# A layer of long convolution and FFN: the last rows stored as 384 and 256 columns, twelve more warm-up products, four row turns issued by ScalarE's queue, and a new order

## The chip, the cores and the metric

The kernel runs on one core of a Trainium2 chip. The metric is the device time of one execution in microseconds, as the median of several runs. Engines are named as the profile names them: PE is TensorE (matmul; PEld is its weight load), DVE is VectorE, ACT is ScalarE, POOL is GpSimd, SP is SyncE, which here only issues DMAs. ScalarE and GpSimd can issue DMAs too; such an instruction stands in the engine's own queue, and what stands behind it waits for it.

## The reference

The inputs are bf16. q, k, v and x are 2048 x 640 (q and x are the same array); the weights of the FFN are 640 x 1728, 640 x 1728 and 1728 x 640.

```
ks = 4                                     # A: long convolution with gates
k_shift = causal convolution of k with shift_k (4 taps a channel)
kv = k_shift * v
y  = irfft(rfft(kv, 2S) * rfft(ssm_k, 2S))[:S] + kv * ssm_D
h  = x + layernorm(x) * y
h2 = h + (silu(n @ w_gate) * (n @ w_up)) @ w_down,   n = layernorm(h)
```

## The kernel before

The sequence is cut into four blocks of 512, and each block into four rows of 128 (one row has one sequence position per partition). The long convolution is done with DFTs of 1024 as matrix products, one per block: the spectra of kv and of the convolution's kernel are formed, multiplied and summed over pairs of blocks, and turned back. Then come the gate, the second layernorm and the FFN of the block.

A block's work has these stages, each with its name in the plan: loads of g (the convolution's kernel), k, v and x; `g` and `k`, where these are turned so that channels lie on partitions (DMA transposes L429 and L520, or PE transposes L539 in block 0), the four taps as products with diagonal matrices (L564) and the product with v; `X` and `G`, the spectra (products L344 of 320 columns, evictions L333); `h`, the window of two spectra; `m`, multiply and add on VectorE (L631, L658); `n`, the first layernorm's statistics (L669, L711, on ScalarE) and norm (L687); `i`, the inverse (VectorE steps L738 to L773, products L793, gate L807 and residual L820); `t`, the second layernorm applied (L719 on VectorE or L722 on ScalarE) and the rows turned (`turn_h`); `f`, the FFN of the block: gate and up products of 512 columns (L903, L980), evictions into sg on ScalarE (L963, with the gate's activation, and L969), products of these on VectorE (L971, L968, L990), and the down products of 320 columns (L1019), a row of 640 columns being a PSUM tile of two halves.

**Row turns.** In blocks 1, 2 and 3 (`HTURN`) the normalised row goes through a DMA transpose into its quarter of the tile hT (L833); in block 0 TensorE transposes it (L840) and ScalarE evicts (L842). The FFN's products L903 read all four quarters at once. In before SP issues every DMA transpose of the kernel, as all other hardware-queue DMAs but the very first (the taps' load).

**The end of a row in the FFN.** In blocks 0, 1 and 2 ScalarE evicts a row (L1025) and GpSimd adds it onto the output by DMA (L1026); with L1025 the row's PSUM tile comes free. In block 3 VectorE adds the row and h (L1035, or L1037 for a part), and SP stores it (L1039). The very last row is done in parts, so that less is behind the last product: 320, 160 and 160 columns (`LASTCUT`, L1005 and L1006), the last parts in a second PSUM tile.

**The order.** Every piece of work is an operation of a plan with a number, an engine and its buffers. The list `ORDER` gives the order in which they are issued (913 of them), and so the order in each engine's queue; buffers are taken from fixed pools in that order (4 PSUM tiles, 11 big tiles, 6 rows, 8 spectra; a row is free again when its turn has landed). A negative number -n-1 is operation n on its other engine (an eviction on VectorE in place of ScalarE). Nothing is reordered at run time; an engine that has to wait holds up all that stands behind.

**Warm-up.** TensorE begins with products of constants (`spin`, L1059) in three groups of 14, 16 and 8 (`WARMUP`): until the taps come, behind the turned taps (L1066), and behind the transposes of k (L539).

SP stops at the end until every DMA has landed (L1209), and then all engines meet.

Of the kernel before, what the change touches and what calls it, by code (L numbers as in the profile page):

```python
# [17 lines left out]
D = 640  # L18
FF = 1728
P = 128  # L20
# [31 lines left out]
WARMUP = (14, 16, 8)  # L52
# [9 lines left out]
LASTCUT = True  # L62
DIAGDVE = 4
ORDER = [
    1, 0, 4, 2, 3, 5, 7, 12, 8, 13, 9, 6, 15, 11, 14, 10, 27, 28, 23, 16, 127, 24, 122, 32, 124, 121, 17, 18, 19, 25, -27, 29, 31,
    -31, 33, -35, 20, 39, -41, 126, 36, -38, 21, 42, 35, 218, 41, 189, 123, 184, -44, 125, 44, 58, 190, 59, 79, 38, 80, 62, -64,
    45, 81, 60, -47, 64, 120, 75, 188, 128, 82, 47, -62, 66, 22, 65, 76, 51, 182, 77, -49, 54, 67, 68, -53, 78, 83, 387, 55, 49,
    187, 84, 261, 260, 53, 186, -70, 389, 56, -51, 71, 85, 96, -58, -73, -87, 100, 97, 73, 70, 101, -75, 262, 92, -94, 98, 99, 87,
    102, 103, 129, 132, 88, 89, 94, 95, 104, 105, 90, 108, 112, 185, 421, 91, 131, 130, 109, 106, 116, 113, 107, 110, 133, 134,
    117, 388, 111, 336, 191, 118, 137, 195, 319, 192, 119, 114, 193, 197, 196, 391, 203, 115, 199, 198, 211, 141, 135, 194, 207,  # L70
    204, 138, 205, 136, 200, 208, 201, 139, 209, 212, 206, 140, 210, 213, 214, 147, 202, 222, 318, 142, 159, 144, 145, 223, 148,
    151, 300, 215, 152, 146, 150, 143, 162, 160, 156, 219, 310, 163, 309, 149, 161, 225, 157, 164, 158, 153, 167, 301, 220, 154,
    166, 168, 396, 224, 155, 165, -227, 299, 398, 399, 221, 227, 397, 228, 229, 390, 243, 244, 169, 231, 235, 230, 239, 232, 217,
    -171, 236, 233, 240, 234, 237, 238, -180, -174, 245, -177, 246, 216, 241, 248, 180, 181, 177, 178, 174, 602, 175, 251, 171,
    249, 172, 263, 400, 264, 394, 311, 242, 266, 247, 395, 312, 303, 302, 253, 304, 305, 183, 265, 259, 315, 255, 256, 306, 313,
    402, 327, 401, 406, 307, 250, 252, 308, 320, 254, 407, 314, 267, 328, 356, 392, 316, 317, 257, 408, 409, 258, 321, 324, 337,
    323, 410, 354, 414, 403, 355, 415, 404, 411, 322, 416, 405, 601, 417, 412, 330, 413, 425, 325, 345, 418, 268, 329, 426, 428,
    332, 420, 333, 326, 331, 431, 334, 600, 429, 269, 422, 432, 335, 271, 280, 457, 346, 427, 270, 277, 273, 278, 423, 424, 274,
    419, 433, 430, 275, 348, 283, 603, 607, 347, 351, 454, 357, 284, 272, 281, 456, 279, 285, 339, 443, 434, 455, 435, 609, 338,
    349, 444, 458, 606, 342, 436, 437, 276, 350, 608, 459, 460, 447, 445, 340, 352, 341, 393, 610, 446, 289, 438, 611, 359, 448,  # L80
    523, 343, 344, 439, 449, 461, 450, 358, 451, 287, 440, 441, 282, 442, 286, 288, 360, 513, 361, 363, 367, 522, 473, 382, 383,
    353, 364, 368, 512, 452, 290, 372, 362, 297, 469, 298, 640, 365, 366, 616, 617, 373, 384, 618, 291, 385, 463, 369, 370, 620,
    619, 374, 624, 377, 625, 621, 295, 293, 453, 378, 375, 292, 626, 622, 462, 465, 470, 464, 467, 474, 623, 379, 294, 296, 612,
    376, 524, 687, 627, 613, 527, 466, 604, 468, 614, 380, 605, 525, 526, 650, 615, 644, 690, 628, 528, 529, 514, 477, 475, 689,
    647, 651, 632, 540, 371, 652, 532, 381, 648, 472, 531, 478, 516, 471, 515, 518, 541, 517, 568, 641, 519, 645, 630, 642, 787,
    533, 785, 629, 649, 536, 534, 691, 476, 631, 646, 569, 542, 686, 535, 493, 570, 633, 567, 549, 643, 520, 530, 480, 479, 485,
    521, 550, 537, 481, 538, 482, 543, 634, 545, 490, 484, 487, 546, 494, 491, 692, 495, 544, 635, 559, 547, 539, 483, 486, 488,
    496, 571, 492, 497, 657, 658, 498, 572, 688, 548, 653, 573, 574, 558, 659, 654, 489, 637, 551, 552, 655, 660, 553, 575, 555,
    639, 730, 554, 656, 576, 636, 561, 666, 560, 500, 556, 595, 502, 674, 501, 557, 596, 729, 499, 577, 564, 562, 731, 563, 578,
    590, 784, 591, 503, 510, 506, 508, 676, 739, 638, 509, 565, 786, 767, 766, 566, 662, 748, 507, 504, 663, 579, 597, 667, 673,  # L90
    511, 661, 664, 505, 592, 749, 665, 668, 669, 593, 675, 670, 678, 386, 671, 677, 598, 740, 672, 580, 581, 585, 757, 586, 582,
    587, 680, 769, 588, 768, 758, 771, 770, 772, 773, 774, 872, 744, 827, 742, 741, 583, 743, 735, 685, 679, 589, 733, 682, 745,
    793, 746, 732, 734, 750, 681, 736, 737, 776, 584, 775, 753, 845, 751, 747, 683, 794, 760, 759, 817, 795, 796, 693, 684, 873,
    754, 599, 777, 778, 738, 781, 874, 763, 752, 694, 695, 762, 755, 863, 788, 707, 780, 761, 844, 756, 710, 779, 696, 702, 764,
    697, 713, 782, 699, 853, 704, 703, 698, 714, 789, 711, 700, 705, 862, 594, 712, 718, 715, 719, 802, 706, 716, 818, 701, 708,
    709, 826, 765, 783, 717, 797, 720, 725, 807, 835, 798, 726, 803, 790, 791, 812, 721, 723, 724, 813, 792, 808, 727, 799, 728,
    722, 814, 815, 816, 804, 871, 809, 805, 819, 820, 829, 800, 801, 828, 823, 832, 836, 821, 822, -825, 847, 864, 865, 868, 825,
    849, 846, 850, 848, 810, 830, 831, 833, 854, 806, 838, 866, 858, 867, 834, 851, 855, 852, 857, 869, 837, 841, 870, 856, 875,
    859, 860, 861, 840, 877, 839, -843, 880, 881, 876, 899, 901, 843, -879, 902, 879, 882, 883, 889, 894, 895, 896, 897, 890, 891,
    892, 884, 905, 885, 893, 898, 908, 909, 886, 900, 887, 903, 906, 888, 910, 911, 904, 907, 912, 913, 811]  # L100
# [33 lines left out]
class Op:  # L134
    def __init__(self, n, eng, ns, fn, name, bufs, deps):
        self.n, self.eng, self.ns, self.fn, self.name, self.bufs, self.deps = n, eng, ns, fn, name, bufs, deps
        self.other = self.rest = None


class Plan:  # L140
    TOOK = {8: 9, 128: 13, 256: 18, 320: 21, 512: 28.5, 640: 33, 1024: 47, 1280: 57, 4096: 160, 5120: 199}
# [39 lines left out]
    def schedule(self, order):  # L181
# [3 lines left out]
        for n in order:  # L185
            op = self.ops[n if n >= 0 else ~n]
            assert op not in done and op.deps <= done
            done.add(op)
            if n < 0:
                op.eng, op.ns, op.fn = op.other  # L190
                if op.rest:
                    op.rest.fn = None
            for b in op.bufs:
                if b.tag is not None and b.at is None:
                    b.at = idle[b.tag].pop(0)
            for b in op.bufs:
                b.left -= 1
                if b.left == 0 and b.tag is not None:
                    idle[b.tag].append(b.at)
# [5 lines left out]
def kernel(ctx: ExitStack, tc: tile.TileContext, A_q, A_k, A_v, A_shift_k, A_ssm_k, A_ssm_D, B_x,  # L205
# [50 lines left out]
    def load(nbytes, packet, fn, w, r=()):  # L256
        return plan.moved("sp", nbytes, packet, fn, r, w)

    def transfer(nbytes, fn, r, w, eng="turn"):
        return plan.moved(eng, nbytes, 256, fn, r, w)  # L260
# [161 lines left out]
    def g_turned(g, drow=None):  # L422
        gT = new("t4")
        if plan.block in GTURN:
# [3 lines left out]
            for r in range(R):  # L428
                transfer(MB / 4, lambda r=r: nc.sync.dma_start(  # L429
                    out=ap(gT)[:, r, :].rearrange("p (c q) -> p c q", c=KT),  # L430
                    in_=ap(by_r).rearrange("q a b -> q (a b)")[:, r * D:(r + 1) * D], transpose=True), [by_r], [(gT, r)])
# [83 lines left out]
    def load_k(j):  # L515
        if j in KTURN or not j and K0TURN:
            kT = new("kT")
            for r in range(R):
                q, e = (nc.scalar, "aturn") if not j and r % 2 else (nc.sync, "turn")
                transfer(MB / 4, lambda r=r, q=q: q.dma_start(  # L520
                    out=ap(kT)[:, :, r, PAD:], in_=block(kk, j)[:, r, :], transpose=True), [], [(kT, r)], e)
# [304 lines left out]
    def turn_h(x, stats):  # L826
        hT = new("hT")
        for r, s in [(r, s) for s, rs in stats for r in rs]:
# [3 lines left out]
            if plan.block in HTURN:  # L832
                transfer(MB / 4, lambda hn=hn, at=at: nc.sync.dma_start(  # L833
                    out=ap(hT)[:, :, at * P:(at + 1) * P], in_=ap(hn), transpose=True), [hn], [(hT, r)])
# [11 lines left out]
    def load_w(gi):  # L846
# [24 lines left out]
        for i, (to, src, lo, n) in enumerate(parts):  # L871
            load(P * KT * n * 2, 2 * n, lambda to=to, src=src, lo=lo, n=n: nc.sync.dma_start(
                out=ap(w)[:, :, to:to + n], in_=cols(src, lo, n)), [(w, i)])
# [5 lines left out]
    def ffn(j, hT, h, end=False, lead=0):  # L879
# [121 lines left out]
        for r in ROWS:  # L1001
# [3 lines left out]
            cuts = [0, 4, 8, NCH] if last and LASTCUT else [0, 5, 10, NCH]  # L1005
            parts = [((0, 1), 0, NH)] if not last else [((0,), 0, NH), ((1,), 0, NH // 2), ((1,), NH // 2, NH // 2)] if LASTCUT else [((0,), 0, NH), ((1,), 0, NH)]  # L1006

            other = new("ps_f") if last and LASTCUT else ps

            def of(hs, to, n):  # L1010
                return [(other if to else ps, frozenset((hf, x) for hf in hs for x in range(to, to + n, NH // 2)))]
# [202 lines left out]
```

## Time and profile before

| what | value |
| --- | --- |
| time, median of three runs | 262.95 us (262.94, 262.95, 263.18) |
| the profiled execution's own time | 262.58 us |
| its span in the profile | 260.9 us (1.68 us lie around it) |
| granted TensorE clock | 1.00 |
| first product of block 0's FFN | 48.91 us |
| first row turn issued, blocks 1, 2, 3 | 101.09, 152.85, 204.63 us |
| first product of block 3's FFN | 213.11 us |
| last product begins, ends | 257.43, 257.66 us |
| w_down's last 80 KB | issued 4.97 us, landed 11.0 us later |

How to read the profile: a page gives busy times and shares of each engine, groups of instructions by line of the kernel, and the chain of work that ended last. Further views give the same for a stretch of time, an instruction's wait, or a queue's DMA issues with the time from issue to landing. A PE instruction's duration contains its latency; products that follow each other start 0.216 us apart for 512 columns and 0.136 us for 320, so the distance of starts is the cost. A number behind an engine's busy time, as in (x909), counts instructions.

### The profile page before, as it was taken

To read this page: it belongs to the slowest core of one execution; us is meant where nothing else is said; L and a number is where in the kernel's file an instruction comes from. 1 tells how busy PE (TensorE), PEld (TensorE's weight loads), DVE (VectorE), ACT (ScalarE), POOL (GpSimd) and SP (SyncE) were. 2 spreads that over 40 slices of the span, in tenths; PEclk is the share of its full clock that TensorE was granted. 3 is DMA by queue.
4 is the path that set the end of the run, shared out by engine and by line. 5 is a ranking of instruction groups with operands and counts; after the bars stand their busy time and mean duration, and the time that the engine had idled before them with its cause. 6 is when DMAs were issued, how large, how long until landed. Compare 5 with 4: busy or idle time off the path is not lost.

```text
span 260.9 us, 4685 instructions
## 1 busy us (share of the span) xinstructions
PE 254.3 (97%) x1800; PEld 158.0 (61%) x1800; DVE 206.4 (79%) x303; ACT 170.1 (65%) x289; POOL 68.7 (26%) x81
## 2 busy tenths in 40 slices
PE   8999999999999999999999999999999999999995
PEld 7877686555675567757554567544446764444674
DVE  5599999999999999999999999999999501032132
ACT  3899999987688983799788975263486133445100
POOL 5140500049965101121015000259950030100000
PEclk9999999999999999999999999999999999999999
DMA  7999967847997899989987959897387284020011
GB/s 257 390 281 256 212 186 189 304 122 143 240 226 127 174 211 288 117 158 291 192 215 115 241 103 212 217 175 197 79 211 193 53 197 54 3 25 0 0 53 50
DMA packets 72482, 44.07 MB, mean 169 GB/s; under 512 B 31174, under 2 KB 69260, under 8 KB 72460
## 3 DMA queue, kind: packets, MB, share of 16 engines
q1 hardware_dynamic: 68210, 37.22, 56.8%
q0 software_dynamic: 4240, 6.56, 16.2%
q8 instruction: 14, 0.23, 0.4%
q14 instruction: 8, 0.07, 0.1%
q10 hardware_dynamic: 10, 0.01, 0.0%
HBM read 30.01 MB, written 4.59 MB: 133 GB/s over the span
## 4 chain that ended last, share of the span: by engine, by line
PE 83%; DVE 9%; ACT 4%; DMA 2%; issue 1%; SPq 0%; DVEq 0%
PE ps L903 40%; PE ps L1019 23%; PE ps L344 5%; PE ps L564 5%; PE ps L980 5%; PE ps L793 3%; DVE S L631 2%; DMA big<-in_A_q_dram 2%; DVE row L807 1%; ACT big L842 1%; ACT big L333 1%; ACT S L333 1%; DVE big L631 1%; DVE S L336 1%; DVE big L738 1%
## 5 line engine op out<-in xcount | busy, mean ns | idle before, releaser
L903 PE MATMUL ps<-big,big 128*128 128x512 bf16 x480 | 108.2, 379 | 0.2 <-ACT big L842 0.2
L903 PEld LDWEIGHTS <-big 128*128 128x128 bf16 x480 | 46.8, 98 | 52.7 <-issue 0.3
L1019 PE MATMUL ps<-wd,tT 128*128 128x320 bf16 (+1 forms) x429 | 60.3, 295 | 0.0
L1019 PEld LDWEIGHTS <-tT 128*128 128x128 bf16 x429 | 41.3, 98 | 16.4 <-issue 0.4
L963 ACT ACTIVATE sg<-ps 128x1024 bf16<-128x1024 f32 (+1 forms) x28 | 26.9, 970 | 20.6 <-PE ps L903 17.5
L344 PE MATMUL ps<-big,WF 128*128 128x320 bf16 x224 | 36.5, 299 | 0.8 <-ACT big L333 0.4
L659 DVE TENSOR_TENSOR S<-S,big 128x2560 bf16<-128x2560 bf16 x23 | 34.3, 1492 | 0.8
L658 DVE TENSOR_TENSOR big<-S,S 128x2560 bf16<-128x2560 bf16 x23 | 34.1, 1483 | 0.0
L969 ACT CAST sg<-ps 128x1024 bf16<-128x1024 f32 (+1 forms) x25 | 24.2, 966 | 10.6 <-PE ps L903 9.5
L971 DVE TENSOR_TENSOR tT<-sg,sg 128x1024 bf16<-128x1024 bf16 (+1 forms) x25 | 16.3, 654 | 15.9 <-ACT sg L969 15.9
L344 PEld LDWEIGHTS <-WF 128*128 128x128 bf16 x224 | 21.7, 98 | 11.7 <-issue 1.2
L669 ACT ACTIVATE row<-big 128x640 bf16<-128x640 bf16 x32 | 23.9, 753 | 2.6 <-DVE big L820 2.5
L1026 POOL DMA_DIRECT2D out_dram<-row x12 | 11.7, 1050 | 47.5 <-ACT row L1025 47.5
L264 POOL DMA_DIRECT2D S<-big x3 | 3.8, 1261 | 63.4 <-DVE S L412 25.2
L564 PE MATMUL ps<-diag,kT 128*128 128x128 bf16 x320 | 19.5, 219 | 0.6 <-ACT kT L543 0.6
L564 PEld LDWEIGHTS <-kT 128*128 128x128 bf16 x320 | 18.6, 98 | 2.2 <-ACT kT L543 0.7
L1025 ACT CAST row<-ps 128x640 bf16<-128x640 f32 x12 | 8.1, 695 | 17.3 <-PE ps L1019 17.1
L333 ACT CAST S<-ps 128x320 bf16<-128x320 f32 (+1 forms) x34 | 17.8, 586 | 1.0 <-PE ps L344 0.5
L722 ACT ACTIVATE row<-big,sm 128x640 bf16<-128x640 bf16 x20 | 17.9, 951 | 0.5 <-DVE sm L676 0.5
L333 ACT ACTIVATE big<-ps 128x640 bf16<-128x640 f32 (+1 forms) x22 | 13.0, 656 | 4.9 <-PE ps L344 4.8
L968 DVE TENSOR_TENSOR tT<-sg,ps 128x1024 bf16<-128x1024 bf16 (+1 forms) x3 | 3.1, 1043 | 15.4 <-PE ps L903 14.4
L980 PE MATMUL ps<-big,big 128*128 128x512 bf16 x60 | 14.7, 379 | 0.0
(94 smaller groups left out, 316.8 us busy)
## 6 DMA issues: line engine op xcount, KB each, us to landing
big<-in_B_w_gate_dram SPq DMA_DIRECT2D x24, 320.0 KB, 4.8
big<-in_B_w_up_dram SPq DMA_DIRECT2D x24, 320.0 KB, 4.5
big<-in_A_q_dram SPq DMA_DIRECT2D x4, 640.0 KB, 5.1
big<-in_A_v_dram SPq DMA_DIRECT2D x4, 640.0 KB, 4.6
big<-in_A_ssm_k_dram SPq DMA_DIRECT2D x4, 640.0 KB, 9.2
wd<-in_B_w_down_dram SPq DMA_DIRECT2D x1, 2080.0 KB
out_dram<-big SPq DMA_DIRECT2D x3, 640.0 KB, 5.0
S<-big POOLq DMA_DIRECT2D x3, 640.0 KB, 6.4
```

Source lines behind the costliest of these rows:

```text
L333: (lambda: nc.scalar.activation(dst(), src(), ACT.Copy, scale=2.0)) if twice else (lambda: nc.scalar.copy(dst(), src())),
L344: nc.tensor.matmul(ap(ps)[:, h, 0:NH], w, ap(src)[:, r, h * NH:(h + 1) * NH], start=(first and i == 0), stop=(last and i == len(rs) - 1), ...
L564: nc.tensor.matmul(line(ap(ps))[:, c * P:(c + 1) * P], ap(kT)[:, c, q, off:off + P], ap(diag)[:, 4 * c + t, :], start=(t == 0), stop=(t == 3))
L658: nc.vector.tensor_mul(flat2(b), X.part(xs), H.part(hs))
L659: f(A.part(dst), A.part(dst), flat2(b))
L669: act(825, lambda r=r, junk=junk: nc.scalar.activation(ap(junk), ap(x)[:, r, :], ACT.Square, scale=D ** -0.5, accum_out=sm(s, 1)[:, r:r + ...
L722: nc.scalar.activation(ap(row), ap(x)[:, r, :], ACT.Identity, bias=sm(s, 5)[:, r:r + 1], scale=sm(s, 4)[:, r:r + 1])
L903: nc.tensor.matmul(of(ps, i), ap(w)[:, k, off:off + P], ap(hT)[:, k, lo:lo + n], start=(k == 0), stop=(k == KT - 1))
L963: act(1010 if wide else 600, lambda: nc.scalar.activation(of(sg), of(*gate), ACT.Silu), [(gate[0], gate[1] + i) for i in range(m)], [sg])
L969: op = plan.add("act", 1010 if wide else 590, lambda: nc.scalar.copy(of(co), of(*up)), psu + [sg], [co] + tt, (), ("dve", 1230 if wide els ...
L980: nc.tensor.matmul(ap(ps)[:, i, :], ap(w)[:, k, off:off + P], ap(hT)[:, k, :], start=(k == 0), stop=(k == KT - 1))
L1019: nc.tensor.matmul(ap(ps)[:, hf, to:to + n], t, ap(wd)[:, c, hf * NH + to:hf * NH + to + n], start=(c == order[0]), stop=(c == order[-1]), ...
```

## The change

Four things, and an order that goes with them.

- `WARMUP`: 18, 16 and 16 products in place of 14, 16 and 8.
- `LASTCUT = 2`: the last row of block 3 is done as 384 and 256 columns, in the two halves of one PSUM tile, cut at the products 0, 5, 10 and 14; one add and one store fewer.
- `ATURN`: a row turn, a turn of k or one of g can be issued by ScalarE's queue where the order says so. It says so for four row turns: one of block 1 (operation 294), one of block 2 (507) and two of block 3 (724, 728).
- `ORDER`: 909 operations in a new order. It also lets four more evictions go to VectorE (two of k and one of kv's spectrum in block 0, one of sg in block 2) and four back to ScalarE, and puts the load of w_down's last 80 KB (operation 184) at SP's 46th place instead of its eighth.

```diff
-WARMUP = (14, 16, 8)
+WARMUP = (18, 16, 16)
-LASTCUT = True
+LASTCUT = 2
+ATURN = ('t', 'k', 'g')
...
-                transfer(MB / 4, lambda hn=hn, at=at: nc.sync.dma_start(
-                    out=ap(hT)[:, :, at * P:(at + 1) * P], in_=ap(hn), transpose=True), [hn], [(hT, r)])
+                def turned_by(q, hn=hn, at=at):
+                    return lambda: q.dma_start(out=ap(hT)[:, :, at * P:(at + 1) * P], in_=ap(hn), transpose=True)
+                transfer(MB / 4, turned_by(nc.sync), [hn], [(hT, r)], other=turned_by(nc.scalar) if "t" in ATURN else None)
...
-            cuts = [0, 4, 8, NCH] if last and LASTCUT else [0, 5, 10, NCH]
-            parts = [((0, 1), 0, NH)] if not last else [((0,), 0, NH), ((1,), 0, NH // 2), ((1,), NH // 2, NH // 2)] if LASTCUT else [((0,), 0, NH), ((1,), 0, NH)]
+            cuts = [0, 4, 8, NCH] if last and LASTCUT == 3 else [0, 5, 10, NCH]
+            first = D - 2 * P
+            parts = [((0, 1), 0, NH, 0)]
+            if last:
+                parts = {0: [((0,), 0, NH, 0), ((1,), 0, NH, NH)], 2: [((0,), 0, first, 0), ((1,), 0, D - first, first)],
+                         3: [((0,), 0, NH, 0), ((1,), 0, NH // 2, NH), ((1,), NH // 2, NH // 2, NH + NH // 2)]}[LASTCUT]
...
-                dve({2 * NH: 820, NH: 490, NH // 2: 325}[n], out_of, of(hs, to, n // len(hs)) + [(h, r)], [(o, (lo, n))])
+                dve(160 + 1.03 * n, out_of, of(hs, to, n // len(hs)) + [(h, r)], [(o, (lo, n))])
```

The part of the new order about block 1's turns (298, 296 and 292 on SP, ~294 written as -295 on ScalarE):

```diff
+    358, 523, 439, 449, 344, 450, 286, 461, 363, 288, 440, 606, 441, 365, 360, 451, 287, 608, 289, 442, 353, 452, 361, 362, 367,
+    368, 290, 382, 364, 366, 297, 383, 473, 291, 616, 617, 293, 372, 469, 618, 522, 512, 514, 619, 295, 373, 374, 298, 453, 463,
+    369, 296, 640, 462, -295, 384, 377, 687, 375, 624, 385, 625, 370, 292, 465, 464, 378, 620, 626, 371, 513, 467, 379, 604, 541,
...
+    701, 808, 803, 845, 854, 708, 797, 709, 873, 717, -792, 812, 813, 386, 783, 871, 720, 798, 723, 721, 725, 792, 727, 799, 804,
+    809, -725, 836, 722, 726, 814, -729, 800, 810, 875, 584, 805, 856, 858, 815, 876, 857, 855, 806, 859, 820, 819, 811, 821, 860,
```

In the list, 297, 291, 293 and 295 are the norms of block 1's rows (L719), 375, 385 and 370 evictions L1025 of block 0's rows, 687 a statistic of block 3's first layernorm (L711), 624 and 620 products L344 of g's spectrum; 720 and 723, 721, 725, 727 are block 3's statistic and norms, 791 (written -792) the sg eviction that goes to VectorE, and 875 the first product of block 3's FFN.

## Prediction

> **What bounds the kernel now.** I read the profile in this order: busy shares, busy time by stretch, the chain of waits behind 190 us, then the row turns and their neighbours on ScalarE.
>
> Page, part 1:
>
> ```profile
> PE 254.3 (97%) x1800; PEld 158.0 (61%) x1800; DVE 206.4 (79%) x303; ACT 170.1 (65%) x289; POOL 68.7 (26%) x81
> ```
>
> Busy time by stretch (length, then PE, PEld, DVE, ACT, POOL, the granted clock, DMA share, GB/s):
>
> ```profile
> 8.00:49.00 41.00, 39.48 (x417) 30.97 (x416) 37.81 (x70) 39.07 (x85) 6.53 (x16) 1.00 0.95 255
> 49.00:190.00 141.00, 141.00 (x909) 82.11 (x909) 139.06 (x164) 102.13 (x165) 51.36 (x48) 1.00 0.87 184
> 190.00:202.00 12.00, 11.99 (x73) 6.67 (x71) 11.90 (x21) 9.88 (x17) 2.99 (x3) 1.00 0.88 219
> 202.00:213.00 11.00, 11.00 (x83) 7.92 (x82) 3.60 (x16) 2.40 (x6) 0.85 (x1) 1.00 0.45 91
> 213.00:257.66 44.66, 44.66 (x264) 24.76 (x261) 9.52 (x13) 12.90 (x15) 2.59 (x3) 1.00 0.18 35
> ```
>
> TensorE has no gap from 49 us to 257.66, and VectorE none to speak of until 202 (139.06 of 141.00). So there are two rows of work without slack in the middle. Anything that stops TensorE for a microsecond after 49 us is paid in full; anything taken off another engine is worth nothing, unless TensorE waits for it. A busy row hides short waits, so I count products in the chain (320 columns: 10 in 1.36 us, 0.136 each):
>
> ```profile
> 194.32 1.25 PE ps L793 x8
> ...
> 197.19 1.51 PE ps L1019 x10
> ...
> 200.62 12.66 PE ps L1019 x92
> ```
>
> These should take 1.09, 1.36 and 12.51: 0.46 us of waits, named by the waits view as L793's weight loads waiting for VectorE's L758 and L773. It is all that a new order can win behind 49 us.
>
> **Row turns.** The four rows of a block are normalised and turned into hT by DMA (L833), and the FFN's first product needs all four. Over all three blocks, then for block 1 alone:
>
> ```profile
> L833 SPq DMA_TRANSPOSE big<-row x12: 1217/1284/2483, 101.1 to 208.8; - x12
> ...
> DMA to landing us min/median/max: 2.6/2.6/6.3
> ```
>
> ```profile
> L833 SPq DMA_TRANSPOSE big<-row x4: 1272/2095/2483, 101.1 to 108.0; - x4
> ...
> DMA to landing us min/median/max: 2.8/3.4/4.0
> ```
>
> A turn holds the issuing queue for 1.2 to 2.5 us (an L872 load: 0.52) and lands 2.6 us or more after its issue begins. Every turn of before (L429, L520, L833) is issued by SP. The change puts one turn of block 1, one of block 2 and two of block 3 on ScalarE's queue, in between SP's: SP, SP, **ACT**, SP in blocks 1 and 2; **ACT**, SP, SP, **ACT** in block 3.
>
> What a turn costs beside a turn of another queue, no row shows. The lower bound: nothing waits; ScalarE is held 1.25 us for each. The upper bound: at each change of queue the turn waits until the other queue's turns have landed, 2.6 us or more, and on ScalarE everything behind it waits too. For the lower end: on one queue turns overlap in flight (the fourth of block 1 is issued at 107.97, the third lands at 109.76), and the rows of hT are apart. For the upper end: turns act as one narrow server. In block 1 each issue starts only when the one before has taken its 2.05 to 2.48 us, four times a load's, and this with SP having nothing else to do. Two queues give that server two streams to keep apart. I take the upper end, as the nearest row is this one.
>
> The Trainium skill, page "DMA: Bandwidth & Descriptors", section "Silent corruption: two transposing streams in flight at once", says that the transposes of SP and those of ACT are two streams, and that the later stream's first one must wait for the earlier stream's full completion. No run of before shows it. By that rule the sum is the one of the upper end; without it, that of rival B.
>
> **The change, part by part.**
>
> *Warm-up products, +4 and +8.* At half clock one takes 0.107 us. Four more end at 2.75, inside the gap that ends with the taps at 2.95; eight more end by 7.6, inside the gap that ends with ScalarE's kT eviction (7.88). Cost 0; if that eviction came 0.3 sooner they would cost 0.3.
>
> *Head, to 49 us.* VectorE takes the kT evictions of ScalarE (0.44 each): TensorE starts block 0's products at 7.96, not 7.88. VectorE and ScalarE set the end of this stretch with the same number of evictions in the same places: −0.03, within 0.15 either way.
>
> *Block 1's turns.* Ahead of the norms now stand two FFN products (L971 0.42, L990 0.41), so the first turn is issued at 101.6 (before: 101.09), the second 2.05 later at 103.7. It lands 2.8 to 4.0 later, 106.5 to 107.7. Only then does ScalarE issue the third (1.28): to 107.8 or 109.0. Behind it on ScalarE is first an n3 statistic (L711, 0.74), then the L1025 eviction (0.69) that frees the PSUM tile for a G3 product (L344): 109.2 to 110.4. Before, these stood so:
>
> ```profile
> 105.63 0.70 ACT L333 CAST big<-ps 128x640 bf16<-128x640 f32 x1
> 107.16 1.30 ACT L333 ACTIVATE big<-ps 128x640 bf16<-128x640 f32 x2 [0.83 <-PE ps L344]
> 108.66 0.69 ACT L1025 CAST row<-ps 128x640 bf16<-128x640 f32 x1 [0.21 <-DMA big<-row]
> ```
>
> TensorE reached that product at 106.41; ten L1019 products (1.36) now come ahead of it and four L344 (0.54) go behind: 107.2. So it stops for 2.0 to 3.2 us; I take **+2.7**. The fourth turn, on SP, waits for ScalarE's landing (109.3 to 111.6) and lands by 112 to 114.2, when the FFN's first product, pushed to 114.5, is only just due: nothing more. If nothing waits, ScalarE's issue ends by 104.8 and the eviction comes 0.9 ahead of its product: 0.
>
> *Block 2's turn.* The same on ScalarE to about 161.4; the last turn lands at 165.3, the first product of the FFN is due at 166.1: 0.
>
> *Late waits.* The inverse's VectorE steps now stand at least 0.67 us ahead of their products (0.25 before): **−0.46**. One sg eviction goes from ScalarE to VectorE (0.57).
>
> *Block 3's turns.* The first row is normed by 205.15 (before 204.57; the added 0.57). ScalarE's turn 205.2, landed 207.8; SP's two at 207.8 and 209.05, landed 211.65; ScalarE's second then, landed 214.25. Before, the FFN's first product began at 213.11; less 0.46 and plus 2.7 it is due at 215.35. VectorE follows TensorE's 2.7 late by an unknown part, 0 to 2.7: the turns end at 214.25 to 216.95. Taking 1.9: 216.15, **+0.8** (0 to 1.6). The three L1025 behind ScalarE's second turn wait with it and free PSUM within that time.
>
> *Tail.* The last rows of before:
>
> ```profile
> 257.00 0.32 DVE L1037 TENSOR_TENSOR row<-ps,big 128x160 bf16<-128x160 f32 x1
> ...
> 257.43 0.23 PE L1019 MATMUL ps<-wd,tail 128*128 128x160 bf16 x1
> 257.70 0.32 DVE L1037 TENSOR_TENSOR row<-ps,big 128x160 bf16<-128x160 f32 x1 [0.37 <-PE ps L1019]
> ```
>
> ```profile
> SPq L1209 <- DMA out_dram<-row: 1.1, 1, 1.1
> ```
>
> Fourteen pairs of 384 and 256 columns instead of 320+160+160 (0.136 + 2 x 0.0695): −0.04. The add of 256 columns, between 160 (0.32) and 320 (0.49): 0.42, +0.10. Its store: +0.06. SP's closing waits are asked for in a fixed order, some 0.06 each. The last store of before is DMA 121 of hardware queues, on the first of eight semaphores, so seven checks follow its landing. With one store fewer it falls on the last semaphore: 7 x 0.062 = −0.43. Together **−0.31**.
>
> *Sum against the profiled execution* (262.58: span 260.9 and 1.68 around it): 262.58 − 0.03 + 2.7 − 0.46 + 0.8 − 0.31 = 265.28. The median shown, 262.95, is 0.37 above that execution: **265.6**.
>
> **Rivals.**
>
> *A, the forecast*: turns of two queues wait for each other. 264.1 (2.0 in block 1, 0 in block 3) to 267.0 (3.2 and 1.6); a landing of 6.3, the longest row, would add 2 more.
>
> *B, the other side*: the queues run side by side. Then nothing stops ScalarE longer than 1.25 us, the third row need not queue behind the second on SP, and the sum is 262.58 − 0.03 − 0.46 − 0.31 = 261.78, or 262.15. It decides at one point: whether ScalarE's turn in block 1 begins before SP's second has landed (106.5 or later). For it: overlapping turns on one queue, 35% of ScalarE idle.
>
> *B2*: as B, but the new order does not remove the late waits, since VectorE has no slack until 202: 262.61.
>
> *C*: as B, but the last 80 KB of w_down, whose load moves from SP's eighth place to the 46th, come too late. Issued at about 88, needed at 93.33; other loads there land in 3.3 to 6.2, its own took 11.0 in before: 99 is 5.5 late, 267.6.
>
> **How the numbers follow.** Chances: A 0.72, B 0.16, B2 0.06, C 0.06. A measurement here can tell about 0.2% (0.53 us) from no change. Faster (under 262.42) is B and a third of B2: 0.18; same is the rest of B2 and a little of B: 0.05; slower is A and C: 0.77. The range takes in B and A with part of a longer landing: 261.9 to 267.4. A alone: 264.1 to 267.4.
>
> **What would show it.** A: a wait on ScalarE in front of its DMA transposes that ends with the landing of SP's; a TensorE gap of 2 to 3 us at an L344 near 107 us; the last turn of block 3 landing after 214. B: ScalarE's turn starting right after its norm, and TensorE without a gap from 49 us to the end. Late waits: L793 pieces of exactly 0.136 per product near 197. Tail: the span ending 2.9 us after the last product's end, not 3.2. Wrong would be above all a stop of TensorE at a place not named here, in the new order's 909 operations.

## The result and the profile after

The changed kernel takes 273.11 us (median of four runs, 272.68 to 273.65) against 262.94 before: ratio 1.0394, 95% interval 1.0381 to 1.0407. The direction was as forecast, the size was not: +10.2 us against +2.7, and outside the range. The profiled execution has a span of 271.2 us, 10.3 more than before.

Busy time by stretch of the changed kernel shows where the time is (length, then PE, PEld, DVE, ACT, POOL, the granted clock, DMA share, GB/s):

```profile
8.00:50.00 42.00, 39.62 (x422) 31.18 (x420) 37.16 (x70) 40.34 (x88) 3.87 (x16) 1.00 0.90 219
...
100.00:110.00 10.00, 8.37 (x62) 5.89 (x61) 9.62 (x20) 2.37 (x6) 1.48 (x2) 1.00 0.92 160
110.00:120.00 10.00, 7.66 (x41) 4.61 (x42) 8.38 (x6) 6.28 (x12) 1.90 (x3) 0.83 0.70 163
...
140.00:150.00 10.00, 8.94 (x47) 4.57 (x47) 9.80 (x15) 7.16 (x11) 3.50 (x4) 1.00 0.78 140
...
218.00:224.00 6.00, 3.77 (x25) 2.29 (x25) 0.00 (x0) 2.48 (x4) 0.44 (x1) 1.00 0.29 55
```

TensorE, without a gap from 49 us on before, now stands still near 108, 145 and 220, and in the first of these the granted clock falls. To price it I subtract from each distance of two starts what the product costs at full clock (0.136 us for 320 columns, 0.216 for 512):

| where | before | after | difference |
| --- | --- | --- | --- |
| first product of block 0's FFN | 48.91 us | 49.88 us | +0.97 |
| stop at 108 us (L1038 to L355) | 0 | 4.1 | +4.1 |
| half clock behind it, 112.3 to 115.5 | 0 | 1.5 | +1.5 |
| stop at 145 (L355 to L995) | 0 | 1.17 | +1.2 |
| stop at 174 (block 2's FFN begins) | 0 | 0.25 | +0.25 |
| waits at 194 to 200 | 0.46 | 0 | −0.46 |
| stop at 220 (block 3's FFN begins) | 0 | 2.33 | +2.3 |
| stop at 266, in the last row | 0 | 0.81 | +0.8 |
| from the last product's start to the end of the span | 3.47 | 3.19 | −0.28 |

Together 10.4, of 10.3 to explain. (In the changed kernel's lines L844 to L847 are the row turn that was L833, L918 was L903, L995 was L980, L1038 was L1019, L1044 was L1025, L724 was L711, L355 and L344 were L344 and L333.)

**Block 1's turns.** ScalarE's timeline and SP's, then TensorE's; the last column in brackets is the idle time before an instruction and what ended it:

```profile
102.43 0.69 ACT L344 CAST big<-ps 128x640 bf16<-128x640 f32 x1 [0.48 <-PE ps L355]
109.44 1.29 ACTq L847 DMA_TRANSPOSE big<-row  x1
110.83 0.74 ACT L724 ACTIVATE row<-big 128x640 bf16<-128x640 bf16 x1 [7.71 <-DMA big<-in_B_w_gate_dram]
...
111.57 1.27 ACT L1044 CAST row<-ps 128x640 bf16<-128x640 f32 x2
```

```profile
102.80 5.13 SPq L847 DMA_TRANSPOSE big<-row  x3
```

```profile
106.85 1.52 PE L1038 MATMUL ps<-wd,tT 128*128 128x320 bf16 x10
112.29 1.23 PE L355 MATMUL ps<-big,WF 128*128 128x320 bf16 x4 [3.92 <-ACT row L1044]
```

SP issues three turns. ScalarE reaches its own at 102.43 and waits in its queue until 109.36, when the third of SP has landed (109.29 in the trace); then come the statistic and two evictions, and with the end of the first of these (112.24) TensorE's product. The name behind 7.71 is misleading: a wait for several is put down to the last that the profile sees, and that load, issued at 107.97, is not what the turn waits for. The queue's own row says it:

```profile
L847 ACTq EVENT_SEMAPHORE  x4: 17/38/6755, 102.4 to 109.4; - x4
```

One of four waits in front of ScalarE's turn lasts 6.755 us. These waits are semaphore instructions in ScalarE's queue: in the kernel's plan no turn depends on another, they come in when the program is built.

**Block 3's turns.**

```profile
213.35 7.95 ACTq L847 DMA_TRANSPOSE big<-row  x2
```

```profile
216.01 2.52 SPq L847 DMA_TRANSPOSE big<-row  x2
```

```profile
222.96 1.24 PE L995 MATMUL ps<-big,big 128*128 128x512 bf16 x4 [2.17 <-DMA big<-row]
```

ScalarE's first turn lands at 215.93 and SP's next is issued at 216.01; SP's second lands at 219.92 and ScalarE's second is issued at 220.07. That is the handover of the forecast, twice, with 0.08 and 0.15 us between landing and issue.

### The profile page after: what moved, and what is told of

Same layout as the page of the kernel before. It is cut to its first block, busy times and chain, and to the rows that moved or that the text cites. A ratio compares the mean times of both kernels' runs of the same rounds, so it can differ in the third digit from the quotient of the medians.

```text
span 271.2 us, 4665 instructions
## 1 busy us (share of the span) xinstructions
PE 255.8 (94%) x1782; PEld 158.9 (59%) x1798; DVE 206.4 (76%) x302; ACT 169.9 (63%) x289; POOL 65.1 (24%) x81
## 4 chain that ended last, share of the span: by engine, by line
PE 54%; DVE 26%; DMA 8%; issue 5%; ACT 4%; SPq 2%; DVEq 0%; ACTq 0%
PE ps L918 32%; PE ps L1038 13%; DMA big<-in_A_ssm_k_dram 4%; DVE S L644 4%; PE ps L355 3%; PE ps L995 3%; DVE big L671 3%; DVE row L820 3%; DMA big<-row 3%; DVE S L672 2%; DVE big L644 2%; PE ps L577 2%; DVE tT L986 2%; SPq L847 1%; DVE S L390 1%
## 5 line engine op out<-in xcount | busy, mean ns | idle before, releaser
L918 PE MATMUL ps<-big,big 128*128 128x512 bf16 x467 | 106.7, 379 | 0.9 <-ACT big L856 0.2
L918 PEld LDWEIGHTS <-big 128*128 128x128 bf16 x480 | 46.8, 98 | 53.4 <-issue 0.7
L1038 PE MATMUL ps<-wd,tT 128*128 128x320 bf16 (+2 forms) x416 | 61.8, 302 | 0.6 <-DVE row L1055 0.6
L1038 PEld LDWEIGHTS <-tT 128*128 128x128 bf16 x416 | 41.1, 99 | 17.8 <-issue 0.8
L355 PE MATMUL ps<-big,WF 128*128 128x320 bf16 x224 | 36.9, 302 | 4.4 <-ACT row L1044 3.9
L355 PEld LDWEIGHTS <-WF 128*128 128x128 bf16 x224 | 21.7, 98 | 15.7 <-issue 5.0
L682 ACT ACTIVATE row<-big 128x640 bf16<-128x640 bf16 x32 | 23.7, 746 | 2.3 <-DMA big<-in_A_q_dram 1.3
L1045 POOL DMA_DIRECT2D out_dram<-row x12 | 11.1, 1241 | 40.3 <-ACT row L1044 40.3
L344 ACT CAST S<-ps 128x320 bf16<-128x320 f32 (+1 forms) x35 | 18.3, 578 | 3.6 <-PE ps L355 2.8
L577 PE MATMUL ps<-diag,kT 128*128 128x128 bf16 x320 | 19.0, 219 | 0.0
L983 DVE TENSOR_TENSOR tT<-sg,ps 128x512 bf16<-128x512 bf16 (+1 forms) x3 | 2.6, 862 | 21.5 <-PE ps L918 19.6
L577 PEld LDWEIGHTS <-kT 128*128 128x128 bf16 x320 | 18.4, 98 | 0.9
L724 ACT ACTIVATE row<-big 128x640 bf16<-128x640 bf16 x16 | 11.8, 737 | 11.1 <-DMA big<-in_B_w_gate_dram 7.7
L995 PE MATMUL ps<-big,big 128*128 128x512 bf16 x57 | 14.7, 379 | 3.3 <-DMA big<-row 2.2
L1044 ACT CAST row<-ps 128x640 bf16<-128x640 f32 x12 | 7.7, 694 | 11.1 <-PE ps L1038 10.4
```

The source lines that it names most:

```text
L344: (lambda: nc.scalar.activation(dst(), src(), ACT.Copy, scale=2.0)) if twice else (lambda: nc.scalar.copy(dst(), src())),
L355: nc.tensor.matmul(ap(ps)[:, h, 0:NH], w, ap(src)[:, r, h * NH:(h + 1) * NH], start=(first and i == 0), stop=(last and i == len(rs) - 1), ...
L577: nc.tensor.matmul(line(ap(ps))[:, c * P:(c + 1) * P], ap(kT)[:, c, q, off:off + P], ap(diag)[:, 4 * c + t, :], start=(t == 0), stop=(t == 3))
L682: act(825, lambda r=r, junk=junk: nc.scalar.activation(ap(junk), ap(x)[:, r, :], ACT.Square, scale=D ** -0.5, accum_out=sm(s, 1)[:, r:r + ...
L918: nc.tensor.matmul(of(ps, i), ap(w)[:, k, off:off + P], ap(hT)[:, k, lo:lo + n], start=(k == 0), stop=(k == KT - 1))
L995: nc.tensor.matmul(ap(ps)[:, i, :], ap(w)[:, k, off:off + P], ap(hT)[:, k, :], start=(k == 0), stop=(k == KT - 1))
```

## The experiments

Thirteen kernels; each ratio is to the kernel before on the same chip.

**1. The four turns back on SP** (e1): 263.88 us, ratio 1.0049 (1.0032 to 1.0066).

```diff
-    369, 296, 640, 462, -295, 384, ...
+    369, 296, 640, 462, 294, 384, ...
```

(and 507, 724 and 728 likewise)

> The changed kernel, with its four ScalarE turns issued by SP again, all else as changed. Theory (the change of queue makes turns wait, and ScalarE's evictions with them): the stops of TensorE near 108 us (4.1, and 1.5 of half clock behind it), 174 (0.25) and 220 (2.3) go, 8.2 in all: 264.9 us, or 263.8 if the 1.2 us stop at 145 hangs on them too. Rival (the new order is the slower one, whoever issues the turns): 270 or more, with the stop near 108 still there.

The stops at 108, 174 and 220 are gone (0.24 is left at the last), the one at 145 stays, at 138 now. The changed kernel takes 9.2 us more than this one. In the two profiles, whose spans differ by 9.1, 7.9 are these stops and the half clock; the other 1.2 is a later start (block 0's FFN begins at 49.88, here at 48.71), which has another cause (runs 12 and 13). So ScalarE's queue costs some 8 of the 10.2 us, and the new order with the new tail, the changed kernel's other parts, 0.8 where the start is on time. The theory's first number missed by that late start; its second, 263.8, came out by luck, as the stop at 145 stayed.

**2. The same four turns in the kernel before** (e2): 269.61 us, ratio 1.026 (1.0227 to 1.0293).

> The kernel before, its order and its tail, with the same four turns (294, 507, 724, 728) issued by ScalarE. Theory: a turn on ScalarE costs only through what waits behind it. Here the third turn of block 1 stands behind the evictions that free PSUM for TensorE, so ScalarE holds back little: 263 to 264 us. Rival (a turn on ScalarE costs 2 to 5 us wherever it stands): 268 to 271.

Here my theory failed, and the rival's number came out. Little waits behind block 1's turn, but the turn itself waits: in ScalarE's queue it stands behind an eviction that begins at 111.31, so it is issued at 111.53 instead of 105.77, and lands at 115.08. TensorE's timeline, and the clock around it:

```profile
112.20 0.71 PE L355 MATMUL ps<-big,WF 128*128 128x320 bf16 x4
115.32 0.58 PE L918 MATMUL ps<-big,big 128*128 128x512 bf16 x1 [2.42 <-DMA big<-row]
116.12 3.21 PE L918 MATMUL ps<-big,big 128*128 128x512 bf16 x8 [0.22 <-issue]
```

```profile
110.00:115.00 5.00, 2.90 (x22) 1.86 (x19) 4.93 (x5) 3.62 (x9) 1.48 (x2) 1.00 0.74 100
115.00:118.50 3.50, 2.96 (x7) 1.20 (x9) 3.46 (x3) 1.44 (x4) 0.86 (x1) 0.55 0.89 245
```

In block 2 SP's first turn lands at 160.00, ScalarE's is issued at 160.07 and, under load, lands 6.57 later; SP's other two wait until 166.66. TensorE stops for 1.4 us there, and for 1.5 in block 3. A turn on ScalarE costs in two ways: what stands behind it waits with it, and it waits for what stands ahead.

**3. The two parts of the last row alone, in the kernel before** (e3): 262.70 us, ratio 0.9992 (0.9982 to 1.0002).

> The kernel before with the last row alone as changed: 384 and 256 columns in one PSUM tile. Theory (the two parts share a tile, so the second part's products wait for the add of the first, 0.8 us, against 0.3 gained behind the last product): 263.4 us. Rival (the prediction's tail, 0.31 gained): 262.6.

No stop in the tail: in that order 18 products of 320 columns stand between the last product of the first part and the first of the second part. From the last product's start to the end of the span it takes 3.2 us, not 3.47. So by the trace the forecast's tail is right (the time alone can't be told from no change), and the 0.8 us of the changed kernel come from its order, in which none stand between.

**4. The small load back** (e4): as e1, with operation 21 behind the constant loads; 263.84 us, ratio 1.0040 (1.0021 to 1.0059).

> As e1_turns_on_sp, with the 1.3 KB load of ssm_D moved on SP from the second place back behind the constant loads, as before. Theory (that small load in front makes q, v and g land 2 us later, and TensorE waits for g until 14.6 us): 0.9 us less than e1_turns_on_sp. Rival (the early turns of k, or the longer warm-up, delay the start): the same as e1_turns_on_sp within 0.2.

As e1: the rival's number. But e1's own profile turned out to have no late start at all (g's first turn at 13.45 us, as before), so there was nothing to take away in it. And e4's profiled execution (265.13 us, one of its two longest) does start late, its FFN at 50.03 us, with the load back. There the sixteen warm-up products of the third group (L1079, before: L1059) still run at half clock, 0.107 us apart; in e1 they start 0.06 apart. Of e4 and of e1:

```profile
7.26 1.02 DVE L556 COPY kT<-ps 128x640 bf16<-128x640 bf16 x2 [0.23 <-PE ps L552]
7.54 1.85 PE L1079 MATMUL ps<-const-bfloat16-1.0 128*128 128x128 bf16 x16
9.23 0.94 PE L577 MATMUL ps<-diag,kT 128*128 128x128 bf16 x14
```

```profile
6.92 1.10 PE L1079 MATMUL ps<-const-bfloat16-1.0 128*128 128x128 bf16 x16 [0.22 <-ACT kT L556]
7.86 4.68 PE L577 MATMUL ps<-diag,kT 128*128 128x128 bf16 x80
```

In e4 the last eviction of kT ends at 8.28, and the taps' products (L577) begin at 9.23. So the longer warm-up, the rival's cause, holds up the start in some executions. Runs 12 and 13 take up the load.

**5 and 6. One block's turns at a time**, from the changed kernel: only 294 on ScalarE (e5), 269.74 us; only 724 and 728 (e6), 266.83 us; one execution each.

> The changed kernel with only block 1's turn (294) left on ScalarE; the other three are SP's again. Theory (each crossing has its own price, and they add): 263.9 of e1_turns_on_sp plus the 4.1 of stop and 1.5 of half clock seen near 108 us: 269.5 us. Rival (the stop near 108 comes from being late at the start, 1 us in the profile of the changed kernel): 264 to 266.

> The changed kernel with only block 3's turns (724 and 728) left on ScalarE. Theory: two crossings, ACT to SP and SP to ACT, each the 2.6 us of a landing, of which TensorE has 1.6 to 2.6 still to wait: 263.9 plus 2.1 = 266.0 us. Rival (the stop at 220 is block 1's lateness handed on): 264.

e5 has the stop near 107 (4.45) and the half clock (1.5), with its start on time, so lateness is not the cause. e6 has a stop of 2.40 at 214, and 0.8 more by a late start. Over e1 they take 5.9 and 3.0 us more; without the late start that is 8.1 together, beside the 7.9 that the stops of all four turns cost. The prices add up.

**7. All of block 3 on ScalarE, in the kernel before** (e7): 265.32 us, ratio 1.0090 (1.0073 to 1.0107).

> The kernel before with all four turns of block 3 on ScalarE, so that the queue does not change within the block. Theory (only a change of queue with turns in flight costs): four turns 1.25 us apart, as on SP, the last landing by 212.5, the FFN on time at 213.1: 263.0 us, within 0.4. Rival (a turn on ScalarE costs by itself, or waits for all that SP has in flight): 1.5 us or more on top, with a stop of TensorE near 213.

The rival's number (2.4 us on top), but not in its place. The turns do not wait for each other, and the last lands at 212.5, in time. But the first stands in front of two sg evictions and waits for its row, and TensorE stops for 2.4 us at 204.8, not at 213:

```profile
202.11 0.19 ACT L682 ACTIVATION_READ_ACCUMULATOR row<-big 128x1 f32 x1
204.85 1.30 ACTq L847 DMA_TRANSPOSE big<-row  x1
206.20 0.60 ACT L978 ACTIVATE sg<-ps 128x512 bf16<-128x512 f32 x1 [3.90 <-DVE row L732]
```

**10. The same, with the first turn behind those evictions** (e10): 262.91 us, ratio 1.0001 (0.9993 to 1.0010).

```diff
-    709, 826, 765, 783, 717, 797, 720, 725, 807, 835, 798, -727, 803, 790, 791, ...
+    709, 826, 765, 783, 717, 797, 720, 725, 807, 835, 798, 803, 790, 791, -727, ...
```

> As e7_block3_all_act, with the first turn moved in the order behind ScalarE's two sg evictions (790, 791), which stood behind it there and reached TensorE 4 us late. Theory (a turn on ScalarE, its queue not changed within the block, costs only what waits behind it while its row is not yet normed): the stop at 204.8 goes, 263.0 us, the time of the kernel before within 0.4. Rival (the turns on ScalarE cost by themselves): 264.5 or more.

```profile
202.13 0.57 ACT L978 ACTIVATE sg<-ps 128x512 bf16<-128x512 f32 x1
202.61 0.56 ACT L984 CAST sg<-ps 128x512 bf16<-128x512 f32 x1
204.79 5.97 ACTq L847 DMA_TRANSPOSE big<-row  x4
```

Four turns in 5.97 us, and no cost. So a turn on ScalarE is not dear by itself: the change of queue within a block is, and what stands next to it.

**8. Two places mended** (e8): as e1, with product 572 ahead of eviction 573 and a PSUM tile of its own for the last 256 columns; 262.45 us, ratio 0.9994 (0.9975 to 1.0014).

```diff
-    547, 491, 787, 492, 488, 489, 657, 658, 653, 573, 654, 572, 501, ...
+    547, 491, 787, 492, 488, 489, 657, 658, 653, 572, 573, 654, 501, ...
...
-            other = new("ps_f") if last and LASTCUT == 3 else ps
+            other = new("ps_f") if last and LASTCUT >= 2 else ps
```

> As e1_turns_on_sp, with two places mended: the product of operation 572 goes ahead of ScalarE's eviction 573 of the other half of its PSUM tile, and the last row's 256 columns get a PSUM tile of their own. Theory (a product that writes one half of a PSUM tile waits for the reader of the other half that stands ahead of it in the order; 1.2 us at 138 and 0.8 at 257): both stops go, 261.9 us, which is below the kernel before. Rival (ScalarE is late there anyway and the stop moves to the next product): 263.0 or more.

The time lies between the two numbers. Both stops are gone from the profile (span 260.3). In e1:

```profile
137.72 0.71 PE L355 MATMUL ps<-big,WF 128*128 128x320 bf16 x4
139.44 1.24 PE L995 MATMUL ps<-big,big 128*128 128x512 bf16 x4 [1.01 <-ACT sg L978]
```

In e8:

```profile
137.51 0.71 PE L355 MATMUL ps<-big,WF 128*128 128x320 bf16 x4
138.05 1.24 PE L995 MATMUL ps<-big,big 128*128 128x512 bf16 x5
```

Against before, the median is lower but the interval includes 1: seven of its twelve runs lie at 262.0 to 262.5, others up to 263.4 and one at 265.2.

**9. The old warm-up in the mended kernel** (e9): 263.24 us, ratio 1.0009 (0.9996 to 1.0021). **11. The new warm-up in the kernel before** (e11): 262.79 us, ratio 0.9996 (0.9987 to 1.0005).

> As e8_mended, with the warm-up of before (14, 16 and 8 products). Theory (the twelve added products fill gaps and cost nothing, or some 0.1 us where the taps come early): the same as e8_mended within 0.2 us. Rival (they hold TensorE up at the start, 0.87 us of products): 0.5 us or more below e8_mended.

> The kernel before with the longer warm-up alone (18, 16 and 16 products). Theory (they fill gaps): the time of the kernel before within 0.2 us. Rival (they hold up the start by a part of their 0.87 us): 263.3 or more against 262.9.

In e11's median the added products cost nothing that can be measured; e4's execution showed the case in which they do. e9 fits neither number, and its profile says why: its q landed 6.6 us after its issue, in e8 4.7. It is the late start again.

**12 and 13. The small load, where the spread shows.** e12 (e8 with the load back): 262.22 us, ratio 0.9975 (0.9960 to 0.9989), ten of twelve runs between 261.94 and 262.29, two at 263.7 and 263.8. e13 (the kernel before with the load second): 263.75, ratio 1.0048 (1.0019 to 1.0077), from 262.69 to 266.21, five of twelve over 265.5.

```diff
-    0, 4, 1, 2, 5, 13, ..., 29, 30, 32, 21, 16, ..., 19, 59, 20, 63, ...
+    0, 4, 1, 2, 5, 13, ..., 29, 30, 32, 16, ..., 19, 59, 20, 21, 63, ...
```

> As e8_mended, with the 1.3 KB load of ssm_D behind the constant loads again. Theory (with that load in the second place q lands at 8.3 in some executions and at 6.3 in others, and g 2 to 3 us late with it): the slower half of e8_mended's and e9_mended_warm's executions goes, 262.2 us, nearly all between 262.0 and 262.6. Rival (the start varies for another reason): spread from 262.0 to 263.7 as with e9_mended_warm.

> The kernel before with that one load moved to the second place on SP, all else as before. Theory: some executions as the kernel before, some 1.0 to 1.3 us longer; a median between 262.9 and 264.2, and a highest over 263.9. Rival: no change, 262.9, all under 263.6.

Both as the theory has it, e13 beyond it. Over all profiled executions: with the load second, g landed 10.0 to 11.7 us after its issue in four of seven, and 8.4 to 8.9 in the others; with it in its old place, 8.3 to 8.9 in all eight. The issues of the first 3.5 us, KB and us from issue to landing, in the kernel before and in the changed one:

```profile
big<-in_A_q_dram SPq DMA_DIRECT2D x1, 640.0 KB, 5.1
...
big<-in_A_ssm_k_dram SPq DMA_DIRECT2D x1, 640.0 KB, 8.6
```

```profile
big<-in_A_q_dram SPq DMA_DIRECT2D x1, 640.0 KB, 6.8
...
big<-in_A_ssm_k_dram SPq DMA_DIRECT2D x1, 640.0 KB, 11.6
```

And the same stretch of 2 us, before and after: the DMA engines are not full (0.92), and move 282 GB/s in place of 403.

```profile
5.00:7.00 2.00, 2.00 (x27) 2.00 (x27) 1.95 (x12) 1.27 (x2) 1.94 (x3) 1.00 1.00 403
```

```profile
5.00:7.00 2.00, 1.96 (x24) 1.84 (x23) 2.00 (x13) 0.56 (x1) 1.94 (x4) 1.00 0.92 282
```

Why one load of 1.3 KB does that, and in some executions only, no run shows. What e13 has beyond the theory its profiled execution (265.60 us) shows. ScalarE's statistic of q (L669, in e13 L682) stands ahead of an eviction of kT (L543, in e13 L556), in the kernel before and in e13:

```profile
6.42 0.74 ACT L669 ACTIVATE row<-big 128x640 bf16<-128x640 bf16 x1
7.06 0.19 ACT L669 ACTIVATION_READ_ACCUMULATOR row<-big 128x1 f32 x1
7.15 0.67 ACT L543 COPY kT<-ps 128x640 bf16<-128x640 bf16 x1
```

```profile
7.99 0.74 ACT L682 ACTIVATE row<-big 128x640 bf16<-128x640 bf16 x1 [1.69 <-DMA big<-in_A_q_dram]
8.63 0.19 ACT L682 ACTIVATION_READ_ACCUMULATOR row<-big 128x1 f32 x1
8.72 0.67 ACT L556 COPY kT<-ps 128x640 bf16<-128x640 bf16 x1
```

```profile
9.45 3.76 PE L577 MATMUL ps<-diag,kT 128*128 128x128 bf16 x37 [2.38 <-ACT kT L556]
```

So TensorE stops for 2.5 us, and the granted clock falls to a half from 9.26 to 12.67 (last section). In the changed order VectorE does this eviction, and its late start comes in the main from g. e12 is faster than both kernels, by 0.25% against before, and has nothing of the change on ScalarE's queue.

## Why the prediction was right and wrong

- **The mechanism** was right: turns of two queues wait for each other. Every handover in the trace shows it (109.29 to 109.44, 112.37 to 112.39, 169.84 to 169.99, 215.93 to 216.01, 219.92 to 220.07 us), and e10, with no handover, costs nothing. The reason that the prediction gave first, turns as one narrow server, is not what these rows show: the turn waits at semaphores of the program. The rule named in the prediction (the Trainium skill, "DMA: Bandwidth & Descriptors", "Silent corruption: two transposing streams in flight at once") agrees with these waits. Whether the turns would corrupt each other without them, or wait all the same, was not tried. B and B2, the rivals without waits, are refuted by the same rows.
- **Block 1's turns, +2.7: mis-sized, 5.6.** The step had ScalarE's turn wait for two SP turns, the second landing at 106.5 to 107.7. In the built program it stands behind all three. In the trace the second lands at 108.55 and the third at 109.29, so the third alone is 0.74 of the 1.4 by which the stop is longer (4.1 for 2.7; e5: 4.45). The rest is that SP's turns begin at 102.80, not 101.6, of which TensorE's own late start takes only 0.97 back, and that ScalarE's instructions behind the wait take 2.9 us, not 2.7. And the step had no price for the clock: after the stop TensorE ran 3.2 us at half clock, in the trace 0.51 of it, 1.5 us more.

```profile
112.30:115.50 3.20, 3.20 (x13) 1.76 (x13) 3.17 (x4) 1.82 (x3) 0.36 (x1) 0.51 0.32 65
```

- **Block 2's turn, 0: 0.25.** The same: the fourth turn lands at 173.86, which is just late.
- **Block 3's turns, +0.8: mis-sized, 2.3.** The chain of three landings was nearly right (forecast 9.05 us from the first issue to the last landing; the stop ends 9.6 behind it). Wrong was the part of TensorE's lateness that VectorE takes over: all of it, not 1.9 of 2.7. The first turn was issued 8.15 us later than forecast, after TensorE had lost 8.0. With no slack in either engine, a lateness is handed on whole, and a later stop adds to an earlier one. By the forecast's own sum that makes 1.6; the longer chain and a first turn 0.15 later still make the rest. e6 shows the same stop (2.40) without the stops of blocks 1 and 2 before it.
- **Head, −0.03: failed, +0.97.** The step looked at evictions and let SP's order of loads pass. In the profile TensorE waits 1.04 us for g, which lands 11.6 us after its issue; the small load moved to second place makes that happen in some executions (e12, e13). Where the start was on time it came earlier than forecast, by 0.2 (e1, 48.71 us) to 0.4 (e8, 48.49). The warm-up's cost of 0 held in e11's median, not in e4's execution.
- **Late waits, −0.46: right.** They are gone in the changed kernel; in e8 one of 0.15 is left.
- **Tail, −0.31: right in itself** (−0.28, and e3), but for a stop of 0.81 that the step had not looked for: two parts share a PSUM tile, so the add of the first waits for the products of the second that stand ahead of it, and the next products wait for that add.

```profile
265.78 0.71 PE L1038 MATMUL ps<-wd,tT 128*128 128x256 bf16 x5
...
266.53 0.56 DVE L1055 TENSOR_TENSOR row<-ps,big 128x384 bf16<-128x384 f32 x1 [0.37 <-PE ps L1038]
267.14 1.03 PE L1038 MATMUL ps<-wd,tT 128*128 128x256 bf16 x8 [0.65 <-DVE row L1055]
```

- **The stop at 145, not foreseen: 1.17.** The same cause, one half of a tile waiting for the reader of the other (e8). In the kernel's plan product 572 does not depend on eviction 573: it writes one half of the tile, and 573 reads the other. The wait is again one of the built program. The forecast said that a stop at an unnamed place would make it wrong; there were two.
- **C, w_down's last load too late**: did not come; no stop names it. (Its lateness was mis-added: 99 less 93.33 is 5.7, not 5.5.)

The sum of the prediction was 2.7. Of the 7.7 that it lacks, 2.9 are block 1's, 1.5 block 3's, 2.0 the two shared tiles, 1.0 the head and 0.25 block 2's.

## What to carry to other kernels

An instruction moved to another engine's queue takes its waits along: price first what it waits for, then everything that stands behind it, and in what the program is built to, not in the list it is written from; DMA transposes of one tile belong on one queue. When two engines have no slack, price a stop with what follows: the clock of TensorE, and the same lateness at the next place that waits. And a product that writes one half of a PSUM tile is worth placing ahead of the eviction of the other half, or in a tile of its own.

## What the runs showed of the hardware

- After stops of 4.1 and 4.45 us TensorE ran at half clock for 3.2 to 3.4 us (a product of 320 columns every 0.27 us), after stops of 2.6 us in e2 and 2.5 in e13 as well; after stops of 2.3 and 2.4 us in the changed kernel, e6 and e7 it did not. The Trainium skill, page "TensorE: Matmul & The Clock Gate", Part 1, puts the return to half clock after an idle window of about 3.4 us that runs freely. The longer stops and the length of the half clock agree; the stops of 2.5 and 2.6 us are shorter than a window, and the measurement decides. What parts the short stops in these traces is where they lie. The clock's changes lie whole steps of 3.41 us apart, and the step ahead of the fall had 1.22 us of TensorE's work in e13 and 0.99 in e2:

```profile
5.85:9.26 3.41, 1.22 (x21) 1.04 (x18) 1.07 (x5) 1.72 (x4) 1.11 (x2) 1.00 0.96 356
9.26:12.67 3.41, 3.22 (x31) 3.23 (x32) 0.81 (x1) 3.41 (x10) 0.27 (x1) 0.50 1.01 362
```

```profile
111.96:115.37 3.41, 0.99 (x8) 0.54 (x7) 3.38 (x3) 2.33 (x6) 0.00 (x0) 1.00 0.82 130
115.37:118.78 3.41, 3.19 (x8) 1.22 (x10) 3.38 (x3) 1.14 (x3) 0.86 (x1) 0.50 1.00 270
```

  The stops that kept the full clock lie across two steps, each with more work; the emptiest is the changed kernel's:

```profile
221.26:224.67 3.41, 1.65 (x7) 0.81 (x9) 0.00 (x0) 2.48 (x4) 1.11 (x3) 1.00 0.25 48
```

  So it is over all thirteen profiles that have the clock's changes, counted in steps between these: each of the 17 falls to half clock, those at the kernel's end included, stands behind a step with 0 to 1.42 us of TensorE's work, and none behind a step with 1.65 or more.

- In the executions with a load of 1.3 KB between loads of 640 KB that start late, the next of these lands up to 2 us later (q 6.3 to 6.8 us after its issue, in the others 4.6 to 5.3); five of twelve executions of e13 were 2.5 us and more longer than the kernel before.
